# Rebuilding split weights on one core: the low words shifted in place by GpSimd, one VectorE operation per half weight instead of two, and a new order

## The chip, the core and the metric

The kernel runs on one core of a Trainium2 chip. The metric is device time in microseconds for one launch. The engines have short names in what follows: PE is TensorE (matrix products), DVE is VectorE, ACT is ScalarE, POOL is GpSimd and SP is SyncE, which only starts transfers. A transfer that ACT starts stands in ACT's own instruction order.

## The reference: what is computed

Clustered attention feeds a feed-forward block. There are 4 batches of 8 heads, 768 positions, head width 64, and 16 centroids per head. A query sees only the keys whose nearest centroid is its own.

```python
mask   = q_assign[:, :, :, None] == k_assign[:, :, None, :]      # nearest centroid
scores = where(mask, q @ k.T / sqrt(64), -1e9)
attn   = softmax(scores) @ v                                     # 4 x 8 x 768 x 64
x      = attn.transpose(0, 2, 1, 3).reshape(3072, 512)
h      = x @ w_in                                                # 512 x 2048
out    = (h * tanh(softplus(h))) @ w_out                         # 2048 x 512
```

## The kernel before, in words

**Order.** All work is cut into small named steps. A class `Plan` (line 27) collects each step with a due time, sorts by it and issues the steps; a step first calls `pl.after(...)` and so issues what it needs (lines 40 to 53). Due times and the shares of the engines come from a table of numbers `T` at line 812. A tile scheduler then lays each engine's instructions in a row from what the steps issue, and `in_turn` (line 102) keeps the table's order for some of ACT's steps. So a changed number in the table can move instructions on every engine.

**Weights.** Each of the two weight matrices arrives as 64-bit values whose two 32-bit words hold one weight between them. They come in 32 halves of 128 x 512 values, numbers 0 to 15 from `w_in` and 16 to 31 from `w_out`. For each half:

- `w_load` (line 213) brings the half into a staging tile `stage`.
- `w_abs` (ACT, line 239) reads the high words and writes a first form of the weight as float32 into a tile `w`.
- `w_f32` (DVE) finishes the float32 in two operations: line 248 shifts `w` left by 3 bits, and line 249 takes the low words, shifts them right by 29 and ORs them in.
- `w_sq` (PE, line 264) sums squares with four products into the tile `gram`.

When all 16 halves of a matrix are in `gram`, `w_scale` (line 270) works out one scale, `ws0r` for `w_in` and `ws1r` for `w_out`, through a short chain on DVE and PE (lines 184, 192 and 195 to 201). Only then can `w_hi` (line 278) multiply each of the 8 tiles of a matrix by the scale, on POOL at line 285 or on ACT at line 287 as the table's share `f_ws` says, and round it to float16 on POOL at line 288. `w_lo` (line 290) subtracts the rounded value from the scaled one on POOL at line 297, which gives the low float16 part. A few tiles go through ACT and DVE at lines 282 and 295 instead.

**Attention.** There are 32 heads in three blocks of 256 queries, each block worked in two halves. PE makes the scores `s` (lines 488 and 493), DVE takes the row maximum `m` (line 503), ACT the exponential `p` (line 510), and DVE or POOL finishes the row sum `l` (lines 520 and 521). In the first eight heads PE transposes `p` (line 549), DVE or ACT copies it out of PSUM (lines 568 and 570), and PE multiplies by the values (line 588). In later heads POOL makes the float16 high part `hl` (line 539), DVE the low part (line 556), a DMA transposes both, and PE multiplies (line 598).

Each head is prepared first. `prep_hi` (line 366) makes the tile `A` from `qk`: either ACT (line 378) or POOL (line 376) does it with the scale inside, or POOL scales `qk` in place first (line 373). `prep_lo` (line 380) makes `B`, the rest, on POOL by a subtraction when `qk` was scaled in place (line 384), otherwise on DVE (line 386). The shares `f_a` and `f_b` decide. Copies `T`, `Z`, `B` and `A` follow, by ACT (line 396) or by DMA (line 398). Line 426 is PE's product with the centroids.

**Feed-forward.** PE multiplies `x` by the float16 weights (lines 655 to 657), ACT makes `u` (line 665), POOL and DVE the two parts of `g` (lines 669 and 677), and PE multiplies by the second matrix (lines 693 to 695). PE takes these pieces between those of the attention.

Of the kernel before, what the change touches and what calls it, by code (L numbers as in the profile page):

```python
# [55 lines left out]
def tile_clustered_attention_mish_ffn(  # L56
# [9 lines left out]
    nc = tc.nc  # L66
# [5 lines left out]
    op1 = pool("operands1", 1)  # L72
# [135 lines left out]
    stage = {}  # L208
# [34 lines left out]
    def w_f32(n):  # L243
        pl.after(("w_abs", n))
        i, hf = divmod(n, 2)
        words = stage[n].bitcast(U32).rearrange("p (n t) -> p n t", t=2)
        f = W[i + 1].bitcast(U32)[:, hf * 512 : (hf + 1) * 512]
        nc.vector.tensor_scalar(f, f, 3, None, op0=ALU.logical_shift_left)
        nc.vector.scalar_tensor_tensor(
            f, words[:, :, 0], 29, f, op0=ALU.logical_shift_right, op1=ALU.bitwise_or  # L250
        )

    def w_sq(n):

# [481 lines left out]
    for n in range(32):  # L736
        p = n // 16
        t = T["w0", p] + T["w_d", p] * (n % 16)
        pl.at(t - T["w_l", p], w_load, n)
        pl.at(t, w_abs, n)  # L740
        pl.at(t + 0.2, w_f32, n)
        pl.at(t + 0.4, w_sq, n)
    for i in range(16):
        p = i // 8
        t = T["w0", p] + T["w_d", p] * 15 + T["ws0", p]
# [56 lines left out]
    for k in range(12):  # L802
        for a in range(2):
            for f in range(8):
                pl.at(ffn(8 * k + 4 * a + f / 2 + T["m2"]), m2, k, a, f)
            t = 8 * k + 4 * a + 4 + T["m2"]
# [3 lines left out]


T = {
    ('f_ws', 0): 0.5,
    ('f_ws', 1): 0.5,
    'direct': 2,
    't0': 2.1861,
    ('f_pl', 0): 0.5,
# [10 lines left out]
    ('dq', 'copy_a'): 0,  # L828
    ('f_copy_t', 0): 0,
    ('f_copy_z', 0): 0.567,  # L830
    ('f_copy_b', 0): 0,
    ('f_copy_a', 0): 0,
    ('f_copy_t', 1): 3,
    ('f_copy_z', 1): 0.874,
    ('f_copy_b', 1): 0,
    ('f_copy_a', 1): 0.193,
    ('f_a', 0): 1,
    ('f_a', 1): 0.239,
    ('f_b', 0): -1,
    ('f_b', 1): 0,  # L840
    'prep_hi': 3.0343,
    'prep_lo': 1.1321,
    'copy_t': 0.5952,
    'copy_z': 0.8008,
    'copy_b': 3.5728,
# [1 line left out]
    'hot_copy': 0.979,  # L847
    'm_store': 0.3296,
    ('f_l', 0): 0,
    ('f_l', 1): 0.434,  # L850
    ('w_l', 0): 0.8888,
    ('w_l', 1): 0.7772,
    'v0': 1.5,
    'v_d': 0.4275,
    ('q_hi', 0): 0.8,
    ('q_lo', 0): 1.4045,
# [5 lines left out]
    ('f_w', 1): 0.363,  # L862
    'lead': 0.5333,
    'units0': 24,
    ('f_d', 0): 0.965,
    ('f_d', 1): 0.732,
    ('f_lo', 0): 0,
    ('f_lo', 1): 0,
    ('f_hi', 0): 0,
    ('f_hi', 1): 1,  # L870
    'grp': 2,
    'mish': 0,
    'O': 1,
    'off0': 25.401,
    'pace': 1.0,
    ('span', 0): 1.1575,
    ('span', 1): 1.0762,
    ('load', 0): -3.8837,
    ('load', 1): 2.8849,
    ('w0', 0): 0.89,  # L880
    ('w0', 1): 9.896,
    ('w_d', 0): 0.3597,
    ('w_d', 1): 0.1964,
    ('ws0', 0): 4.1159,
    ('ws0', 1): 1.7919,
# [6 lines left out]
    'put': 2.3669,  # L892
    ('scores', 0): 0.4,
    ('rowmax', 0): 0.9821,
    ('expo', 0): 2.0645,
    ('recip', 0): 0.7,
    ('scores', 1): 1.8591,
    ('rowmax', 1): 1.6368,
# [41 lines left out]
```

## Time and profile before

The median of three runs is 977.86 us, from 976.33 to 979.1.

| of the profiled execution | |
|---|---|
| its own time | 978.06 us |
| span in the trace | 976.3 us |
| mean granted TensorE clock | 0.981 |
| start of the first product of the feed-forward (line 655) | 208.18 us after the span's start |

Times of a row are microseconds from the span's start unless a unit says otherwise. In a table of windows, each engine has its busy time and its count of instructions in brackets, and `PEclk` is the part of full speed that PE was granted. In a group of instructions stand the line, the engine, the operation and the tiles as out<-in; then the total busy time, the mean of one in nanoseconds, and the idle time just before them with what ended it. In a timeline a row is the start, the length, the instruction, how many of it follow each other, and in square brackets the idle time before it and what ended that.

### The profile page before, as it was taken

Reading aid. Unit: us, or ns where it says so; the run is one execution under the profiler, and the core shown is the slowest. Engines: PE = TensorE matmul, PEld = TensorE weight load, DVE = VectorE, ACT = ScalarE, POOL = GpSimd, SP = SyncE. Lnnn points to the kernel's source line nnn. Section 1 sums busy time; section 2 is a strip of 40 time slices with the busy share of each in tenths; the row PEclk is TensorE's granted clock in tenths of the full one; section 3 lists DMA queues with packets and bytes.
Section 4 is the critical chain, followed back from the end, with each engine's and each line's share of the span. In section 5 each row is a group of like instructions: output and inputs, shape, how many; then the busy total and the mean of one; then the engine's idle time right before and its main releaser. Section 6 shows DMA issues by size and latency. Waiting matters only on the chain. (4 is left out here: it accounts for less than half of the span.)

```text
span 976.3 us, 17239 instructions
## 1 busy us (share of the span) xinstructions
PE 918.5 (94%) x6481; PEld 676.3 (69%) x6481; DVE 644.9 (66%) x1162; ACT 562.2 (58%) x938; POOL 410.0 (42%) x543
## 2 busy tenths in 40 slices
PE   3997789999999999999999999999999999999998
PEld 3765567777667767767777767676777777666663
DVE  6988987887777667866776667866777676211010
ACT  3776367767766656566676665557666665211111
POOL 3226679644444335535434334434434344211010
PEclk9999779999999999999999999999999999999999
DMA  9733732266777866767867667666577565100000
GB/s 360 236 96 90 207 92 61 70 114 129 140 146 138 151 118 139 141 122 148 129 139 134 155 124 144 111 130 142 122 139 123 116 117 111 31 12 22 12 12 21
DMA packets 250323, 115.85 MB, mean 119 GB/s; under 512 B 229632, under 2 KB 229632, under 8 KB 250240
## 3 DMA queue, kind: packets, MB, share of 16 engines
q1 hardware_dynamic: 238272, 82.50, 43.2%
q10 hardware_dynamic: 11968, 32.25, 12.0%
q8 instruction: 51, 0.84, 0.4%
q14 instruction: 32, 0.26, 0.1%
HBM read 35.68 MB, written 6.29 MB: 43 GB/s over the span
## 5 line engine op out<-in xcount | busy, mean ns | idle before, releaser
L510 ACT ACTIVATE p<-s,m 128x768 f32<-128x768 f32 x192 | 172.8, 900 | 132.6 <-DVE m L503 101.7
L656 PE MATMUL h<-x,w 128*128 128x256 f16 x768 | 209.7, 273 | 0.6 <-POOL x L637 0.6
L655 PE MATMUL h<-x,w 128*128 128x256 f16 x768 | 210.1, 274 | 0.1
L657 PE MATMUL h<-x,w 128*128 128x256 f16 x768 | 210.1, 274 | 0.0
L556 DVE SCALAR_TENSOR_TENSOR hl<-p,l,hl 128x768 f16<-128x768 f32 x144 | 152.3, 1058 | 72.7 <-POOL hl L539 72.4
L503 DVE TENSOR_REDUCE m<-s 128x1 f32<-128x768 f32 x192 | 181.2, 946 | 10.0 <-PE s L493 8.4
L539 POOL TENSOR_SCALAR hl<-p,l 128x768 f16<-128x768 f32 x144 | 132.7, 922 | 125.2 <-ACT p L510 47.5
L677 DVE SCALAR_TENSOR_TENSOR g<-u,mscg,g 128x512 f16<-128x512 f32 x96 | 75.8, 792 | 139.8 <-POOL g L669 139.0
L669 POOL TENSOR_SCALAR g<-u,mscg 128x512 f16<-128x512 f32 x96 | 80.8, 842 | 173.7 <-ACT u L665 149.0
L693 PE MATMUL O<-w,g 128*128 128x512 f16 x384 | 146.8, 382 | 2.9 <-POOL g L669 2.1
L695 PE MATMUL O<-w,g 128*128 128x512 f16 x384 | 146.2, 381 | 0.4 <-DVE g L677 0.4
L694 PE MATMUL O<-w,g 128*128 128x512 f16 x384 | 146.2, 381 | 0.0
L488 PE MATMUL s<-A,B 128*128 128x384 f32 x384 | 123.3, 402 | 14.9 <-ACT p L510 12.7
L665 ACT ACTIVATE u<-h,msch 128x512 f32<-128x512 f32 x96 | 65.7, 687 | 97.9 <-PE h L657 94.6
L493 PE MATMUL s<-Z,T 80*128 80x384 f32 x384 | 101.3, 345 | 2.8 <-ACT T L467 2.8
L598 PE MATMUL o<-pt,v 128*128 128x256 f16 x864 | 102.7, 273 | 0.6 <-DMA pt<-hl 0.4
L520 POOL TENSOR_SCALAR l<-l 128x1 f32<-128x1 f32 x129 | 40.5, 314 | 142.7 <-ACT p L510 139.5
L598 PEld LDWEIGHTS <-v 128*128 128x128 f16 x864 | 83.8, 98 | 16.6 <-issue 1.7
L655 PEld LDWEIGHTS <-w 128*128 128x128 f16 x768 | 75.2, 98 | 20.6 <-issue 6.0
L488 PEld LDWEIGHTS s<-A,B 128*128 128x128 f32 x384 | 64.1, 194 | 33.5 <-ACT p L510 18.5
L656 PEld LDWEIGHTS <-w 128*128 128x128 f16 x768 | 75.2, 98 | 15.5 <-issue 1.4
L657 PEld LDWEIGHTS <-w 128*128 128x128 f16 x768 | 75.2, 98 | 15.0 <-issue 5.4
(184 smaller groups left out, 1324.0 us busy)
## 6 DMA issues: line engine op xcount, KB each, us to landing
qk<-in_qk_dram ACTq DMA_DIRECT2D x32, 384.0 KB, 4.2
stage<-in_w_out_dram ACTq DMA_DIRECT2D x16, 512.0 KB, 4.0
vraw<-in_vP_dram SPq DMA_DIRECT2D x16, 384.0 KB, 4.5
out_dram<-osb SPq DMA_DIRECT2D x24, 256.0 KB, 2.7
B<-T ACTq DMA_DIRECT2D x30, 192.0 KB, 4.3
A<-A SPq DMA_DIRECT2D x25, 192.0 KB, 4.8
stage<-in_w_in_dram SPq DMA_DIRECT2D x8, 512.0 KB, 8.9
stage<-in_w_in_dram ACTq DMA_DIRECT2D x8, 512.0 KB, 4.5
```

What stands on the lines that cost most here:

```text
L488: nc.tensor.matmul(s[:, j, :384], st["B", n][:, q0 : q0 + P], st["A", n][:, j * 384 : (j + 1) * 384], start=True, stop=False,)
L503: nc.vector.tensor_reduce(m, st["s", i, a][:, :, :384], axis=AX.XY, op=ALU.max, negate=True)
L510: in_turn(nc.scalar.activation(p.rearrange("p (n x) -> p n x", n=2), st["s", i, a][:, :, :384], AF.Exp, bias=st["m", i, a], scale=1.0, acc ...
L539: nc.gpsimd.tensor_scalar(t[:, 0], p, r, 1.0, op0=ALU.mult, op1=ALU.mult)
L556: nc.vector.scalar_tensor_tensor(t[:, 1], p, r, t[:, 0], op0=ALU.mult, op1=ALU.subtract)
L598: nc.tensor.matmul(o[:, s * 256 : s * 256 + 256], vst[b, h // 2][:, c, h % 2].rearrange("p g d -> p (g d)"), st["pt", 2 * m + s][:, :, c + ...
L655: nc.tensor.matmul(o, wh, xh, start=(c == 0), stop=False)
L656: nc.tensor.matmul(o, wh, xl, start=False, stop=False)
L657: nc.tensor.matmul(o, wl, xh, start=False, stop=(c == 3))
L693: nc.tensor.matmul(o, gh, wh, start=(f == 0 and fi == 0), stop=False)
L694: nc.tensor.matmul(o, gh, wl, start=False, stop=False)
L695: nc.tensor.matmul(o, gl, wh, start=False, stop=(f == 7 and fi == 1))
```

## The change

In `w_f32` POOL now works on the low words in place, in the staging tile, as integers read and written through a multiply and a minimum: each low word is multiplied by 2 to the minus 29, which leaves its upper three bits, and limited to 7. DVE then makes the float32 in one operation that shifts `f` left by 3 and ORs in the low words. The lines after 250 have a number one lower than before.

```diff
     def w_f32(n):
         pl.after(("w_abs", n))
         i, hf = divmod(n, 2)
-        words = stage[n].bitcast(U32).rearrange("p (n t) -> p n t", t=2)
+        low = stage[n].bitcast(U32).rearrange("p (n t) -> p n t", t=2)[:, :, 0]
         f = W[i + 1].bitcast(U32)[:, hf * 512 : (hf + 1) * 512]
-        nc.vector.tensor_scalar(f, f, 3, None, op0=ALU.logical_shift_left)
-        nc.vector.scalar_tensor_tensor(
-            f, words[:, :, 0], 29, f, op0=ALU.logical_shift_right, op1=ALU.bitwise_or
-        )
+
+        nc.gpsimd.tensor_scalar(low, low, 2.0**-29, 7.0, op0=ALU.mult, op1=ALU.min)
+        nc.vector.scalar_tensor_tensor(f, f, 3, low, op0=ALU.logical_shift_left, op1=ALU.bitwise_or)
...
 T = {
-    ('f_ws', 0): 0.5,
-    ('f_ws', 1): 0.5,
+    ('f_ws', 0): 0.061,
+    ('f_ws', 1): 1,
...
-    ('f_b', 1): 0,
+    ('f_b', 1): 1,
```

The table has some twenty changed numbers in all. What they do to the counts of instructions:

| work | before | after |
|---|---|---|
| DVE operations that finish the float32 of a half | 64 | 32 |
| POOL operations on low words | 0 | 32 |
| scaling of `w_in` tiles: POOL, ACT | 4, 4 | 0, 8 |
| scaling of `w_out` tiles: POOL, ACT | 3, 3 | 6, 0 |
| `qk` scaled in place on POOL (line 373) | 8 | 32 |
| `A` from `qk`: POOL with the scale inside, ACT | 6, 18 | 0, 24 |
| `B`: POOL (line 384), DVE (line 386) | 8, 24 | 32, 0 |
| `B` copied: ACT, DMA | 0, 30 | 6, 24 |
| row sums (line 520): POOL, DVE | 129, 63 | 150, 42 |

PE has the same products, and in nearly the same order from the first product of the feed-forward on.

The first place is DVE where the first `w_out` halves become float32, beside the attention of the first batch. `stage` is the half with its two words per weight, `w` its float32. Before:

```order
L248 TENSOR_SCALAR w_1060<-w_1060 128x512
L249 SCALAR_TENSOR_TENSOR w_1060<-stage_1019,w_1060 128x512
L568 COPY pt_998<-q_0_3_994 128x384
L503 TENSOR_REDUCE m_0_1172<-s_0_1167 128x1
L248 TENSOR_SCALAR w_1060<-w_1060 128x512
L503 TENSOR_REDUCE m_1_1216<-s_1_1211 128x1
L249 SCALAR_TENSOR_TENSOR w_1060<-stage_1021,w_1060 128x512
L248 TENSOR_SCALAR w_1097<-w_1097 128x512 x2
L521 RECIPROCAL l_1_1073<-l_1_1073 128x1
L249 SCALAR_TENSOR_TENSOR w_1097<-stage_1033,w_1097 128x512
```

After, at the corresponding place:

```order
L502 TENSOR_REDUCE m_0_1199<-s_0_1194 128x1
L567 COPY pt_898<-q_1_3_1036 128x384
L250 SCALAR_TENSOR_TENSOR w_1111<-w_1111,stage_1029 128x512
L502 TENSOR_REDUCE m_1_1245<-s_1_1240 128x1
L567 COPY pt_1065<-q_0_3_1061 128x384
L250 SCALAR_TENSOR_TENSOR w_1111<-w_1111,stage_1045 128x512
L567 COPY pt_990<-q_1_3_1167 128x384
L250 SCALAR_TENSOR_TENSOR w_1178<-w_1178,stage_1079 128x512
```

The shifts are gone from the row, one operation per half is left, and it reads a low word that POOL has written.

The second place is POOL at the same time in the program, from where the first scale is known. Before:

```order
L285 TENSOR_SCALAR w_323<-w_323,ws0r 128x1024
L285 TENSOR_SCALAR w_490<-w_490,ws0r 128x1024
L285 TENSOR_SCALAR w_603<-w_603,ws0r 128x1024
L285 TENSOR_SCALAR w_760<-w_760,ws0r 128x1024
L288 TENSOR_SCALAR w_275<-w_276 128x1024
L520 TENSOR_SCALAR l_1_1073<-l_1_1073 128x1
L297 TENSOR_TENSOR w_275<-w_276,w_275 128x1024
L288 TENSOR_SCALAR w_276<-w_323 128x1024
L297 TENSOR_TENSOR w_276<-w_323,w_276 128x1024
```

After, where the first float16 weight is made:

```order
L249 TENSOR_SCALAR stage_1238<-stage_1238 128x512
L383 TENSOR_TENSOR B_1226<-qk_1081,A_1173 128x768
L249 TENSOR_SCALAR stage_1259<-stage_1259 128x512
L519 TENSOR_SCALAR l_1_1339<-l_1_1339 128x1
L249 TENSOR_SCALAR stage_1269<-stage_1269 128x512
L287 TENSOR_SCALAR w_275<-w_276 128x1024
L249 TENSOR_SCALAR stage_1288<-stage_1288 128x512
L372 TENSOR_SCALAR qk_1430<-qk_1430,scq 128x768
L296 TENSOR_TENSOR w_275<-w_276,w_275 128x1024
```

POOL scaled and rounded `w_in` while the `w_out` halves were being finished; now its work on the `w_out` halves stands ahead of the first rounding, and the scaling is not in its row.

The third place is ACT, where it multiplies the `w_in` tiles by `ws0r`. Before:

```order
L510 ACTIVATE p_0_1042,l_0_1043<-s_0_1035,m_0_1040 128x768
L239 ACTIVATE w_1060<-stage_1019 128x512
L398 DMA B_1003<-T_975 64x768
L287 ACTIVATE w_276<-w_276,ws0r 128x1024
L287 ACTIVATE w_428<-w_428,ws0r 128x1024
L510 ACTIVATE p_1_1072,l_1_1073<-s_1_1065,m_1_1070 128x768
```

After, from the second of the eight scalings to the next exponential (ahead of the first scaling stands another exponential):

```order
L286 ACTIVATE w_401<-w_401,ws0r 128x1024
L286 ACTIVATE w_475<-w_475,ws0r 128x1024
L286 ACTIVATE w_561<-w_561,ws0r 128x1024
L286 ACTIVATE w_673<-w_673,ws0r 128x1024
L286 ACTIVATE w_740<-w_740,ws0r 128x1024
L286 ACTIVATE w_839<-w_839,ws0r 128x1024
L286 ACTIVATE w_926<-w_926,ws0r 128x1024
L227 DMA stage_1288<-in_w_out_dram 128x512
L239 ACTIVATE w_1343<-stage_1269 128x512
L569 COPY pt_1212<-q_1_0_1376 128x384
L239 ACTIVATE w_1343<-stage_1288 128x512
L509 ACTIVATE p_0_1407,l_0_1408<-s_0_1400,m_0_1405 128x768
```

The scalings on ACT were four, in two pairs with an exponential between; now they are eight, in one block, and the last two line 239 of `w_out` and a copy stand between the block and the next exponential.

More of the change, by code (lines that the diff above doesn't have):

```diff
@@ L830 @@
     ('f_copy_z', 0): 0.567,
-    ('f_copy_b', 0): 0,
+    ('f_copy_b', 0): 1,
     ('f_copy_a', 0): 0,
     ('f_copy_t', 1): 3,
-    ('f_copy_z', 1): 0.874,
+    ('f_copy_z', 1): 0.994,
     ('f_copy_b', 1): 0,
@@ L837 @@
     ('f_a', 0): 1,
-    ('f_a', 1): 0.239,
+    ('f_a', 1): 0,
     ('f_b', 0): -1,
-    ('f_b', 1): 0,
+    ('f_b', 1): 1,
     'prep_hi': 3.0343,
-    'prep_lo': 1.1321,
+    'prep_lo': 2.673,
     'copy_t': 0.5952,
@@ L849 @@
     ('f_l', 0): 0,
-    ('f_l', 1): 0.434,
-    ('w_l', 0): 0.8888,
+    ('f_l', 1): 0.294,
+    ('w_l', 0): 1.4353,
     ('w_l', 1): 0.7772,
-    'v0': 1.5,
+    'v0': 1.214,
     'v_d': 0.4275,
@@ L864 @@
     'units0': 24,
-    ('f_d', 0): 0.965,
+    ('f_d', 0): 0.566,
     ('f_d', 1): 0.732,
@@ L868 @@
     ('f_lo', 1): 0,
-    ('f_hi', 0): 0,
+    ('f_hi', 0): 0.425,
     ('f_hi', 1): 1,
@@ L875 @@
     'pace': 1.0,
-    ('span', 0): 1.1575,
+    ('span', 0): 1.634,
     ('span', 1): 1.0762,
     ('load', 0): -3.8837,
-    ('load', 1): 2.8849,
+    ('load', 1): 2.8855,
     ('w0', 0): 0.89,
-    ('w0', 1): 9.896,
-    ('w_d', 0): 0.3597,
+    ('w0', 1): 9.386,
+    ('w_d', 0): 0.5318,
     ('w_d', 1): 0.1964,
-    ('ws0', 0): 4.1159,
-    ('ws0', 1): 1.7919,
+    ('ws0', 0): 4.606,
+    ('ws0', 1): 1.1124,
     ('ws1', 0): -0.216,
@@ L894 @@
     ('rowmax', 0): 0.9821,
-    ('expo', 0): 2.0645,
+    ('expo', 0): 1.3834,
     ('recip', 0): 0.7,
```

## Prediction

> **What bounds the kernel now.** I read the page first, for the share of each engine and the slices of the span.
>
> ```profile
> PE 918.5 (94%) x6481; PEld 676.3 (69%) x6481; DVE 644.9 (66%) x1162; ACT 562.2 (58%) x938; POOL 410.0 (42%) x543
> PE   3997789999999999999999999999999999999998
> PEclk9999779999999999999999999999999999999999
> ```
>
> PE is at nine tenths nearly everywhere. The exceptions are the first slice and slices 4 to 6, each 24.4 us long, where the granted clock dips too. I cut that part into windows, beside the steady part and the end.
>
> ```profile
> 86.00:98.00 12.00, 6.38 (x52) 4.15 (x48) 9.78 (x15) 9.15 (x15) 10.96 (x10) 0.93 0.42 111
> 98.00:104.00 6.00, 3.73 (x26) 3.17 (x27) 5.89 (x10) 2.45 (x5) 2.56 (x3) 0.56 0.61 206
> 104.00:116.00 12.00, 9.50 (x79) 6.53 (x77) 12.00 (x15) 4.17 (x8) 10.82 (x9) 1.00 0.66 199
> 116.00:128.00 12.00, 8.21 (x38) 6.66 (x38) 10.97 (x18) 7.07 (x14) 7.35 (x8) 0.54 0.79 215
> 128.00:140.00 12.00, 10.43 (x80) 7.54 (x78) 11.87 (x18) 6.43 (x13) 6.97 (x8) 0.89 0.31 84
> 140.00:208.20 68.20, 65.09 (x458) 50.42 (x459) 56.78 (x125) 50.54 (x100) 49.61 (x60) 0.97 0.27 66
> 208.20:830.00 621.80, 608.75 (x4364) 454.93 (x4364) 446.23 (x773) 407.19 (x649) 274.06 (x360) 1.00 0.69 132
> ```
>
> The columns are PE, weight loads, DVE, ACT, POOL, then clock and DMA. From 208 us on PE is busy 98% (608.75 of 621.8) at full clock. Between 86 and 140 us it is not: DVE is busy 50.51 of 54 us, and PE has the clock at 0.54 to 0.56 in 18 of them. What PE waits for there, from the view of waits between 86 and 141 us:
>
> ```profile
> PE gram L264 <- DVE w L249: 13.8, 7, 3.7
> ```
>
> So in this stage DVE's float32 conversion of the `w_out` halves ends last. The groups of DVE in that window, and then the same two lines from 0 to 86 us:
>
> ```profile
> L249 DVE SCALAR_TENSOR_TENSOR w<-stage,w 128x512 uint32<-128x512 uint32 x16 | 19.0, 1195 | 0.1
> L248 DVE TENSOR_SCALAR w<-w 128x512 uint32<-128x512 uint32 x16 | 17.1, 1075 | 1.1 <-ACT w L239 1.0
> ...
> L249 DVE SCALAR_TENSOR_TENSOR w<-stage,w 128x512 uint32<-128x512 uint32 x16 | 11.5, 718 | 0.1
> L248 DVE TENSOR_SCALAR w<-w 128x512 uint32<-128x512 uint32 x16 | 8.5, 533 | 0.4
> ```
>
> The same 32 operations cost 36.1 us here and 20.0 us there. The timelines of DVE, POOL and PE show why:
>
> ```profile
> 30.40 0.43 DVE L248 TENSOR_SCALAR w<-w 128x512 uint32<-128x512 uint32 x1
> 30.86 0.69 DVE L249 SCALAR_TENSOR_TENSOR w<-stage,w 128x512 uint32<-128x512 uint32 x1
> 94.10 2.01 DVE L249 SCALAR_TENSOR_TENSOR w<-stage,w 128x512 uint32<-128x512 uint32 x1
> 96.03 3.51 DVE L248 TENSOR_SCALAR w<-w 128x512 uint32<-128x512 uint32 x2
> 93.44 2.12 POOL L297 TENSOR_TENSOR w<-w,w 128x1024 f16<-128x1024 f32 x1
> 97.10 2.17 POOL L297 TENSOR_TENSOR w<-w,w 128x1024 f16<-128x1024 f32 x1
> 100.27 0.61 PE L264 MATMUL gram<-w 128*128 128x128 bf16 x4 [3.66 <-DVE w L249]
> ```
>
> The first two rows are the bare prices, 0.43 and 0.69 us. Beside POOL's subtraction of 2.1 us the same lines take 2.01 and 1.76 us (3.51 for two). PE then stands 3.66 us, and the window from 98 us has the clock at 0.56.
>
> **What the change is worth, part by part.** The sum is made against the profiled execution, 978.06 us, of which the span is 976.3; it lies 0.2 us above the median of the runs.
>
> *The stage of the `w_out` halves.* PE's full-clock work from 86 to 140 us is its busy time times the clock: 6.38 x 0.93 + 3.73 x 0.56 + 9.50 x 1.00 + 8.21 x 0.54 + 10.43 x 0.89 = 31.2 us of 54. The loss is 22.8 us. After the change DVE has 50.51 - 36.1 = 14.4 us of other work there and 16 operations of the kind of line 249. At the bare 0.69 us they make 11.0 us, and DVE needs 25.4 us where PE needs 31.2; even at 1.0 us each DVE needs 30.4. What makes them dear now, POOL's scaling and rounding of `w_in`, stands behind POOL's work on the halves in the new order, as the second place of the order shows. So PE ends last there and the loss goes: -22.8 us. If half of it stays, since DVE has other work in bursts, the gain is 11.4; this is one bound.
>
> *POOL's new operation.* 32 of 128 x 512 with a stride of two words; the trace of before has none. Its rows of elementwise work on POOL are these:
>
> ```profile
> L669 POOL TENSOR_SCALAR g<-u,mscg 128x512 f16<-128x512 f32 x96 | 80.8, 842 | 173.7 <-ACT u L665 149.0
> L373 POOL TENSOR_SCALAR qk<-qk,scq 128x768 f32<-128x768 f32 x8 | 7.2, 905 | 14.6 <-PE as L426 12.1 <-DMA qk<-in_qk_dram 2.4
> L384 POOL TENSOR_TENSOR B<-qk,A 128x768 fp32r<-128x768 f32 x8 | 15.3, 1913 | 0.3
> ```
>
> By size line 373 gives 905 x 512 / 768 = 603 ns from below and line 384 gives 1275 ns from above. I take 0.75 us between the two, nearer to line 669 (0.842), which has the same size. 32 x 0.75 = 24 us, 12 for each matrix. In the `w_out` stage POOL loses at least the scaling and rounding, so it is covered: 0. If the cover is gone, DVE waits 12 us there; that is a rival below.
>
> The Trainium skill, page "GPSIMD Engine Reference", section "8. Key points", says that for elementwise work DVE is structurally about twice as fast. By that an operation on POOL would take 2 x 0.43 = 0.86 us, an estimate, and the sum would be the same as long as POOL is not what ends last.
>
> *ACT's block of eight.* This is a new wait. The order has the eight multiplications by `ws0r` in one piece, with two line 239 and one copy before the next exponential; nothing else on ACT can pass. The rows of ACT for these:
>
> ```profile
> L287 ACT ACTIVATE w<-w,ws0r 128x1024 f32<-128x1024 f32 x4 | 4.4, 1148 | 2.1 <-DMA Z<-B 2.1
> L239 ACT ACTIVATE w<-stage 128x512 f32<-128x512 f32 x32 | 20.9, 671 | 2.2 <-DMA stage<-in_w_out_dram 2.2
> L510 ACT ACTIVATE p<-s,m 128x768 f32<-128x768 f32 x192 | 172.8, 900 | 132.6 <-DVE m L503 101.7
> L570 ACT COPY pt<-q 128x384 f32<-128x384 f32 x48 | 22.8, 475 | 17.0 <-DVE onehot L456 8.0 <-PE o L588 5.1 <-PE q L549 3.2
> ```
>
> 8 x 1.148 + 2 x 0.671 + 0.475 + 0.900 = 11.9 us. Ahead of it ACT waits for `ws0r`, whose DVE chain has a row maximum (0.95), a copy (0.55), a conversion and small operations between its steps, which I put at 4 us to 5.5 us: ACT gives no exponential for about 16.5 us. PE has, in its order in that time, the square sums of five tiles, two score pairs, twelve transposes and six products with the centroids. The means of these groups between 86 and 208 us:
>
> ```profile
> L549 PE MATMUL q<-ident,p 128*128 128x128 f32 x183 | 31.3, 300 | 1.8 <-DVE pt L568 1.7
> L488 PE MATMUL s<-A,B 128*128 128x384 f32 x62 | 19.4, 395 | 1.3 <-ACT p L510 1.3
> L493 PE MATMUL s<-Z,T 80*128 80x384 f32 x62 | 16.8, 354 | 0.0
> L264 PE MATMUL gram<-w 128*128 128x128 bf16 x64 | 7.5, 248 | 13.8 <-DVE w L249 13.8
> L426 PE MATMUL as<-C,qk 128*128 128x128 f32 x60 | 9.1, 310 | 1.4 <-ACT p L510 1.4
> ```
>
> By busy time over count: 36 to 40 square products at 0.117 = 4.5, four score products at 0.313 and four at 0.271 = 2.3, twelve transposes at 0.171 = 2.1, six at 0.152 = 0.9: about 10 us. PE stands for some 6.5 us, 9 where the chain is longer, and the clock then costs more. Before, each loss on PE of 3.66 us was followed by a window of 6 us at 0.56, where 3.73 x 0.44 = 1.6 us go; with several waits I take 3. I set the whole at +12, with bounds 0 (PE has more queued than I count) and +17 (nothing but the clock recovers).
>
> *The start.* ACT's first line 467 stands behind a load:
>
> ```profile
> 19.80 0.98 ACT L467 ACTIVATE T<-oh,mbi,msc 16x768 fp32r<-16x768 bf16 x1 [10.80 <-DMA vraw<-in_vP_dram]
> 20.84 1.26 PE L493 MATMUL s<-Z,T 80*128 80x384 f32 x4 [2.80 <-ACT T L467]
> ```
>
> In the new order that load no longer stands ahead. At most PE's 2.80 us go; POOL's subtraction, which ends with it, holds some. I take -1.5 us, between 0 and -2.8.
>
> *The steady part.* For each of 22 later heads POOL gains a scaling and a subtraction, 0.905 + 1.913 = 2.82 us, 62 us in all. POOL is busy 274 of 621.8 us, so 348 are free. DVE loses line 386 and ACT gains some copies, but PE is busy 98% there: 0, with a loss as a rival.
>
> The sum: -22.8 + 12 - 1.5 = -12.3, and 978.06 - 12.3 = 965.8; I say **966 us**. The first product of line 655 then starts near 196 us, not at 208.18.
>
> **Rivals.**
>
> *ACT's block is covered.* PE's queue is long enough, since PE takes scores of the next blocks meanwhile. For it: from 86 to 208 us PE stood only 1.3 us ahead of line 488 for `p`, with four scalings on ACT in that time. Then 978.06 - 22.8 - 1.5 = 953.8 us, **954**. Chance 0.16.
>
> *POOL takes back what DVE saves.* The 16 new operations on POOL beside the conversions hold up DVE's remaining one, as line 297 does now; 16 x 0.75 = 12 us, which with the block on ACT uses up the gain: 965.8 + 12 = 977.8, **978**, no change. For it: line 248 takes up to 1.76 beside POOL and 0.43 alone. Against it: line 249, which reads two tensors, costs 0.718 in the mean up to 86 us. Chance 0.15. By the Trainium skill, page "GPSIMD Engine Reference", section "8. Key points", POOL shares its SBUF interfaces with DVE, with contention for DVE operations in a 2-port mode or with two inputs in SBUF; the rows at 94.10 and 96.03 us agree, 2.01 for 0.69 and 1.76 for 0.43.
>
> *Slower: POOL's queue in the steady part.* The scaling and the subtraction stand in POOL's row ahead of the float16 parts of the probabilities (line 539), on which DVE already waits:
>
> ```profile
> L556 DVE SCALAR_TENSOR_TENSOR hl<-p,l,hl 128x768 f16<-128x768 f32 x144 | 152.3, 1058 | 72.7 <-POOL hl L539 72.4
> ```
>
> Its point of decision: 12.3 us over 22 heads is 0.56 us per head of 2.82, a fifth. Where a third of the 62 us reaches PE, 20.7 us, the time is 965.8 + 20.7 = **986 us**. Against it: PE has waited at 98% busy with DVE standing those 72 us. Chance 0.16.
>
> **How the numbers follow.** The forecast has 0.53, its own range 957 to 975 (the block from +3 to +17, the start's bounds, part of the stage's loss left). The range over all cases goes from 952, a little below the first rival, to 980, past the second; what is left out is the third and the lower edge, under 0.2. What a measurement of this kernel can tell from no change is 0.3%, 2.9 us: faster is below 975. Faster: 0.53 + 0.16 = 0.69, less a little for the forecast's upper edge, 0.68. Same: the second rival and that edge, 0.16. Slower: 0.16.
>
> **What would show it.** Right: line 250 at 0.7 to 0.8 us in the `w_out` halves, `gram` waiting for it under 4 us, a block of 9.2 us on ACT with a wait of PE for `p` of 6 us or more behind it, line 655 starting by 198 us, and from there to the end the same 768 us. Wrong: PE in the steady part under 97% with waits on `hl` or `B` (third rival); line 250 over 1.2 us (second); no wait behind ACT's block (first).

## The result, and the profile after

The change made the kernel slower: 988.43 us in the median (987.15 to 994.34, four runs) against 978.48 us of the kernel before beside it. The ratio is 1.0117, with a 95% interval of 1.0092 to 1.0141. The forecast was 966 us with a range of 952 to 980. The profiled execution took 987.43 us, with a span of 985.6. The first product of line 655 (now 654) starts at 209.12 us, for 208.18 before and about 196 in the forecast; from there to the end it is 776.5 us, for 768.1 before.

The first part of the page of the kernel after, and its slices:

```profile
PE 918.4 (93%) x6481; PEld 675.1 (68%) x6481; DVE 624.1 (63%) x1091; ACT 573.6 (58%) x954; POOL 541.9 (55%) x631
PE   4898669998999999999999999899999999999997
PEclk8799889999999999999999999999999999999999
POOL 8985888997654546754555456544645544111010
```

PE has the same work (918.4 us, 918.5 before). POOL went from 410.0 to 541.9 us and is now at eight or nine tenths in nearly all of the first ten slices. To find the 9.3 us by which the span grew, the span is cut into five stages. PE's loss in a stage is its length minus busy time times granted clock. Windows of the kernel before, then of the kernel after, with the columns in the same order as in the prediction. The clock has two digits, which matters over 510 us: in the kernel before it is 0.97 from 340 to 390 us, in the kernel after 1.00. So the table takes its last row of the kernel before in two windows (50 - 47.88 x 0.97, and 460 - 453.25 for the rest at full clock):

```profile
0.00:86.00 86.00, 65.00 (x445) 50.52 (x447) 69.63 (x165) 50.30 (x100) 28.38 (x63) 0.94 0.63 207
86.00:140.00 54.00, 38.25 (x271) 28.05 (x267) 50.51 (x72) 29.27 (x54) 38.66 (x34) 0.81 0.55 158
140.00:190.00 50.00, 47.38 (x331) 36.75 (x332) 39.30 (x92) 36.12 (x73) 41.73 (x48) 0.97 0.19 49
190.00:340.00 150.00, 145.33 (x1072) 110.99 (x1069) 113.69 (x197) 105.43 (x173) 63.31 (x90) 1.00 0.74 139
340.00:850.00 510.00, 501.13 (x3565) 371.27 (x3564) 354.60 (x618) 321.89 (x515) 223.36 (x289) 1.00 0.66 126
...
340.00:390.00 50.00, 47.88 (x328) 34.85 (x327) 34.48 (x65) 30.81 (x51) 21.61 (x30) 0.97 0.65 126
```

```profile
0.00:86.00 86.00, 66.51 (x448) 51.64 (x448) 62.56 (x140) 52.18 (x101) 68.81 (x81) 0.90 0.59 199
86.00:140.00 54.00, 38.14 (x276) 29.51 (x274) 36.58 (x83) 37.76 (x64) 42.57 (x35) 0.87 0.50 151
140.00:190.00 50.00, 46.63 (x341) 35.03 (x336) 33.12 (x73) 32.67 (x68) 45.98 (x49) 1.00 0.19 48
190.00:340.00 150.00, 139.48 (x1010) 105.06 (x1011) 114.36 (x184) 101.41 (x167) 97.76 (x110) 0.99 0.68 133
340.00:850.00 510.00, 497.27 (x3548) 369.14 (x3546) 358.80 (x589) 328.95 (x526) 269.78 (x335) 1.00 0.66 127
```

| PE's loss, us | before | after | difference |
|---|---|---|---|
| 0 to 86 | 24.9 | 26.1 | +1.2 |
| 86 to 140 | 23.0 | 20.8 | -2.2 |
| 140 to 190 | 4.0 | 3.4 | -0.6 |
| 190 to 340 | 4.7 | 11.9 | +7.2 |
| 340 to 850 | 10.3 | 12.7 | +2.4 |

The differences add up to 8.0 of the 9.3 us; the rest lies behind 850 us and in the rounding. Two things stand out. From 86 to 140 us DVE has 13.9 us less to do (36.58 for 50.51) and PE loses nearly as much as before. And the loss comes after 190 us, where the forecast had none.

The groups of POOL's new operation, over the whole run, and of DVE's one from 86 to 141 us:

```profile
L249 POOL TENSOR_SCALAR stage<-stage 128x512 uint32<-128x512 uint32 x32 | 65.2, 2039 | 6.3 <-DMA stage<-in_w_out_dram 3.0 <-DMA stage<-in_w_in_dram 1.0
L250 DVE SCALAR_TENSOR_TENSOR w<-w,stage 128x512 uint32<-128x512 uint32 x16 | 12.6, 790 | 1.8 <-POOL qk L372 1.7
```

DVE's operation costs 0.79 us, as forecast (0.7 to 0.8). POOL's costs 2.04 us where 0.75 was taken, and 65.2 us in all instead of 24.

The block on ACT, with PE's wait behind it; the two rows of ACT are the eight scalings. The rows of POOL and DVE at that time stand below them:

```profile
118.55 4.25 ACT L286 ACTIVATE w<-w,ws0r 128x1024 f32<-128x1024 f32 x4
122.71 4.25 ACT L286 ACTIVATE w<-w,ws0r 128x1024 f32<-128x1024 f32 x4
127.23 2.12 POOL L296 TENSOR_TENSOR w<-w,w 128x1024 f16<-128x1024 f32 x1
127.61 2.30 DVE L250 SCALAR_TENSOR_TENSOR w<-w,stage 128x512 uint32<-128x512 uint32 x1 [1.68 <-POOL qk L372]
129.96 0.61 PE L263 MATMUL gram<-w 128*128 128x128 bf16 x4 [3.64 <-DVE w L250]
```

Line 239 of the last two halves stands behind the block (the first of them ends at 127.52 us, nearest to DVE's start, though the profile names POOL's line 372, which ended at 127.27), DVE behind it, and PE behind DVE: 3.64 us. But the block is only a part of this wait: DVE's operation took 2.30 us instead of 0.69 beside POOL's subtraction, so 1.6 of the 3.64 us are POOL's.

Last, the chain that makes the first scale: the row maximum of line 184, PE's product of line 192, and the reciprocal, at which the scale is known. The last row is the last subtraction that makes float16 weights. Before, then after:

```profile
74.99 0.16 DVE L184 TENSOR_REDUCE ws0m<-wss 128x1 f32<-128x16 f32 x1
...
80.36 0.28 PE L192 MATMUL ws0p<-ws0m,ones 128*128 128x1 f32 x2
...
86.64 0.16 DVE L201 RECIPROCAL ws0r<-ws0r 128x1 f32<-128x1 f32 x1
...
186.14 2.38 POOL L297 TENSOR_TENSOR w<-w,w 128x1024 f16<-128x1024 f32 x1
```

```profile
88.99 0.16 DVE L184 TENSOR_REDUCE ws0m<-wss 128x1 f32<-128x16 f32 x1
...
111.28 0.35 PE L192 MATMUL ws0p<-ws0m,ones 128*128 128x1 f32 x2 [0.32 <-DVE xf L628]
...
115.90 0.17 DVE L201 RECIPROCAL ws0r<-ws0r 128x1 f32<-128x1 f32 x1
...
223.65 2.58 POOL L296 TENSOR_TENSOR w<-w,w 128x1024 f16<-128x1024 f32 x1
```

The scale comes 29 us later, and the weights' float16 parts end at 226.2 us and not at 188.5. Of the 29 us, 14 are the row maximum, which comes later. The rest comes from the place of its product in PE's row: line 192 starts 22.3 us behind the maximum, for 5.4 before. With POOL's operation in the short form and the same rows (h1, below) it starts 21.2 us behind, at 112.25 after 91.01 us, so this belongs to the new order and not to POOL's price. No run moves that product.

The float16 work now runs beside the first feed-forward and the first later heads. From 190 to 240 us it holds up a DVE operation on the values (line 332), which took 1.00 us at 194.01 and takes 2.88 beside POOL's subtraction:

```profile
196.77 2.13 POOL L296 TENSOR_TENSOR w<-w,w 128x1024 f16<-128x1024 f32 x1
...
196.83 2.88 DVE L332 SCALAR_TENSOR_TENSOR v<-vraw,vs1r,v 128x768 f16<-128x768 f32 x1 [0.43 <-POOL v L331]
```

DVE's operation on the probabilities (line 555) is longer there too, 1.43 us in the mean for 1.04. But its long ones stand beside other work of POOL; the longest, 2.57 us, is beside line 383, the subtraction for a later head.

### The profile page after: what moved, and what is told of

Read it like the earlier page. It is cut to its first block, busy times and chain, and to the rows that moved or that the text cites. A ratio compares the mean times of both kernels' runs of the same rounds, so it can differ in the third digit from the quotient of the medians.

```text
span 985.6 us, 17186 instructions
## 1 busy us (share of the span) xinstructions
PE 918.4 (93%) x6481; PEld 675.1 (68%) x6481; DVE 624.1 (63%) x1091; ACT 573.6 (58%) x954; POOL 541.9 (55%) x631
## 5 line engine op out<-in xcount | busy, mean ns | idle before, releaser
L555 DVE SCALAR_TENSOR_TENSOR hl<-p,l,hl 128x768 f16<-128x768 f32 x144 | 158.5, 1102 | 74.6 <-POOL hl L538 74.2
L502 DVE TENSOR_REDUCE m<-s 128x1 f32<-128x768 f32 x192 | 181.3, 946 | 22.5 <-PE s L492 20.8
L668 POOL TENSOR_SCALAR g<-u,mscg 128x512 f16<-128x512 f32 x96 | 77.8, 811 | 173.3 <-ACT u L664 153.4
L676 DVE SCALAR_TENSOR_TENSOR g<-u,mscg,g 128x512 f16<-128x512 f32 x96 | 78.3, 818 | 143.8 <-POOL g L668 143.7
L519 POOL TENSOR_SCALAR l<-l 128x1 f32<-128x1 f32 x150 | 52.9, 353 | 101.2 <-ACT p L509 94.6
L656 PEld LDWEIGHTS <-w 128*128 128x128 f16 x768 | 75.3, 98 | 13.8 <-issue 4.0
```

The source lines that it names most:

```text
L502: nc.vector.tensor_reduce(m, st["s", i, a][:, :, :384], axis=AX.XY, op=ALU.max, negate=True)
L555: nc.vector.scalar_tensor_tensor(t[:, 1], p, r, t[:, 0], op0=ALU.mult, op1=ALU.subtract)
L656: nc.tensor.matmul(o, wl, xh, start=False, stop=(c == 3))
```

## The experiments

The first theories were these. A: POOL's operation was mis-sized, and a POOL that is full up to 130 us costs the time. B: POOL's scaling and subtraction for the later heads cost it. C: ACT's block of eight costs it. D, added with the second set: the new order costs it, whatever the operation costs. Theories E to G stand in the expectations.

All results, each with its ratio to the kernel before on the same chip:

| run | median, us | ratio, 95% interval |
|---|---|---|
| the kernel after | 988.43 | 1.0117, 1.0092 to 1.0141 |
| e1_short_op | 990.38 | 1.0110, 1.0090 to 1.0131 |
| e2_order_alone | 995.64 | 1.0177, 1.0154 to 1.0199 |
| e3_op_alone | 995.57 | 1.0161, 1.0137 to 1.0185 |
| h1_after_held_short | 988.64 | 1.0112, 1.0094 to 1.0129 |
| h2_before_held_min | 1015.80 | 1.0380, 1.0357 to 1.0403 |
| h3_before_held_mul | 977.79 | 0.9997, 0.9984 to 1.0011 |
| h4_before_held_out | 976.53 | 0.9983, 0.9968 to 0.9998 |
| h5_after_heads_on_dve | 987.65 | 1.0088, 1.0063 to 1.0113 |
| h6_after_block_split | 991.06 | 1.0125, 1.0105 to 1.0144 |
| h7_before_loads_on_sp | 976.50 | 0.9982, 0.9968 to 0.9997 |
| h8_after_all_three | 991.08 | 1.0129, 1.0107 to 1.0151 |
| t1_before_tiny_convert | 968.00 | 0.9883, 0.9863 to 0.9903 |
| t3_before_no_load_wait | 977.71 | 0.9985, 0.9971 to 1.0000 |
| t4_before_both | 963.84 | 0.9842, 0.9810 to 0.9873 |
| b1_before_heads_on_pool | 1004.19 | 1.0254, 1.0230 to 1.0278 |
| r1_after_no_load_wait | 985.08 | 1.0063, 1.0046 to 1.0081 |
| r2_before_out_sp | 976.64 | 0.9974, 0.9960 to 0.9989 |

Nine of these seventeen runs lie outside every range that was set for them: e1, e2, e3, h2, h6, h8 and b1 above the highest, t1 and t4 between two.

### First set: the operation, the order, and the operation's forms

e1_short_op:

```diff
-        nc.gpsimd.tensor_scalar(low, low, 2.0**-29, 7.0, op0=ALU.mult, op1=ALU.min)
-        nc.vector.scalar_tensor_tensor(f, f, 3, low, op0=ALU.logical_shift_left, op1=ALU.bitwise_or)
+        nc.gpsimd.tensor_scalar(low[:, :192], low[:, :192], 2.0**-29, 7.0, op0=ALU.mult, op1=ALU.min)
+        nc.vector.scalar_tensor_tensor(f, f, 3, low, op0=ALU.logical_shift_left, op1=ALU.bitwise_and)
```

> POOL's operation works on 192 of the 512 low words, and DVE's operation ANDs where it ORed, so that every value stays finite: the weights are not the reference's, DVE's operation has the same size, and POOL's costs about 2.04 x 192 / 512 = 0.77 us, the size that the prediction had taken. Theory A (the POOL operation was mis-sized, and POOL full up to 130 us is what costs the time): most of the loss goes, 962 to 976 us. Theory B (POOL's scaling and subtraction of the later heads costs the time): little changes, 982 to 990 us. Theory C (the order with ACT's block of eight costs it): 980 to 988.

e2_order_alone is the kernel after with the old body of `w_f32`; e3_op_alone is the kernel before with the new one.

> The new table with the old two DVE operations and no POOL operation. Theory A: POOL is free again, so near the kernel before or a little better, 970 to 982 us. Theory B: the later heads still load POOL, 983 to 990. Theory C: the block of eight is still there and DVE has its old load, 985 to 995.

> The old table with the new pair of operations. Theory A: POOL has 65 us more in a stage of 140 us in which it had 67 us of work, which leaves it nearly full and delays the scaling and rounding of the weights: 980 to 995 us. Theory B: the later heads are as before, so 965 to 979. Theory C: no block of eight, 965 to 979.

All three are slower than the kernel before by 1.1 to 1.8%, and the first is no faster than the kernel after. But a change in an operation's length also moves the order that the scheduler lays, so each of these changes two things at once. They refute no theory by themselves; they show that the new table is slower still without its operation (e2), and the old table slower with it (e3), each in the order that the scheduler then lays.

p1_forms (one execution, so its total time is not compared) adds to the kernel before, on a tile `z` of 128 x 1024 words whose contents are no weights, six rounds of:

```diff
+        G(ue, ue, 2.0**-29, 7.0, op0=ALU.mult, op1=ALU.min)      # L823
+        G(uc, uc, 2.0**-29, 7.0, op0=ALU.mult, op1=ALU.min)      # L824, no stride
+        G(e, e, 1.0, 7.0, op0=ALU.mult, op1=ALU.min)             # L825, float32
+        G(c, c, 1.0, 7.0, op0=ALU.mult, op1=ALU.min)             # L826, float32, no stride
+        G(c, c, 1.0, 1.0, op0=ALU.mult, op1=ALU.mult)            # L827
+        G(o, ue, 2.0**-29, 7.0, op0=ALU.mult, op1=ALU.min)       # L828, not in place
+        G(uo, e, 2.0**-29, 7.0, op0=ALU.mult, op1=ALU.min)       # L829
+        G(ue, ue, 2.0**-29, 1.0, op0=ALU.mult, op1=ALU.mult)     # L830
```

> The kernel before with 48 POOL operations of 128 x 512 at its end, six of each of eight forms, which only lengthen its tail. It asks what makes the operation cost 2.04 us: integers, the stride of two words, the minimum, or the work in place. If integers: 32-bit integer forms about 2 us at either stride and float forms 0.6 to 0.9. If the stride: strided forms about 2 us in both types. If the minimum: only the form with two multiplications is short.

Its groups on POOL from 940 us on:

```profile
L828 POOL TENSOR_SCALAR z<-z 128x512 f32<-128x512 uint32 x6 | 12.1, 2020 | 0.5
L825 POOL TENSOR_SCALAR z<-z 128x512 f32<-128x512 f32 x6 | 11.8, 1972 | 0.5
L829 POOL TENSOR_SCALAR z<-z 128x512 uint32<-128x512 f32 x6 | 11.8, 1969 | 0.5
L826 POOL TENSOR_SCALAR z<-z 128x512 f32<-128x512 f32 x6 | 11.5, 1920 | 0.5
L823 POOL TENSOR_SCALAR z<-z 128x512 uint32<-128x512 uint32 x5 | 10.2, 2032 | 0.4
L824 POOL TENSOR_SCALAR z<-z 128x512 uint32<-128x512 uint32 x5 | 9.6, 1920 | 0.4
L830 POOL TENSOR_SCALAR z<-z 128x512 uint32<-128x512 uint32 x6 | 3.9, 644 | 0.5
L827 POOL TENSOR_SCALAR z<-z 128x512 f32<-128x512 f32 x6 | 3.7, 620 | 0.4
```

It is the minimum. Every form that has it takes 1.92 to 2.03 us, integers or not, with a stride or without; the two with a second multiplication take 0.62 and 0.64. Other operations in its place were not measured.

### Second set: one thing at a time, in a held order

To change an operation's length and nothing else, the program is built twice. The first build is the kernel as it is, and each engine's row is noted; in the second, with the edit, every instruction waits for its predecessor in that row:

```python
for engine, names in ORDER.items():          # rows of the first build
    names = [n for n in names if n in made and str(made[n].engine) == engine]
    for x, y in zip(names, names[1:]):
        tc.add_manual_dep(made[y], x, no_sync, reason="held order")
```

An instruction that the edit moves to another engine is placed there by the scheduler; all others stay where they were. Such runs are called held. The code above is shortened. No run holds the rows without any edit; h3 and t3, held on the kernel before, lie within 0.2% of it.

h1_after_held_short, on the kernel after:

```diff
-        nc.gpsimd.tensor_scalar(low, low, 2.0**-29, 7.0, op0=ALU.mult, op1=ALU.min)
+        nc.gpsimd.tensor_scalar(low, low, 2.0**-29, 1.0, op0=ALU.mult, op1=ALU.mult)
```

> The kernel after, with each engine's row of instructions held exactly as it is, and only the limit to 7 replaced by a multiplication by 1, which the probe of forms measured at 0.64 us in place of 2.0; a low word may round up to 8, which changes a weight's last bits. Theory A (the POOL operation was mis-sized): POOL has some 44 us less before 130 us, so most of the loss goes, 962 to 978 us. Theory D (the new order costs the time whatever the operation costs): 983 to 990 us.

h2_before_held_min and h3_before_held_mul, on the kernel before, and h4_before_held_out, which does it for `n >= 16` alone (shortened; `low` is `words[:, :, 0]`):

```diff
-        nc.vector.tensor_scalar(f, f, 3, None, op0=ALU.logical_shift_left)
-        nc.vector.scalar_tensor_tensor(f, low, 29, f, op0=ALU.logical_shift_right, op1=ALU.bitwise_or)
+        nc.gpsimd.tensor_scalar(low, low, 2.0**-29, 7.0, op0=ALU.mult, op1=ALU.min)   # h2
+        nc.gpsimd.tensor_scalar(low, low, 2.0**-29, 1.0, op0=ALU.mult, op1=ALU.mult)  # h3, h4
+        nc.vector.scalar_tensor_tensor(f, f, 3, low, op0=ALU.logical_shift_left, op1=ALU.bitwise_or)
```

> The kernel before with every engine's row held, except that DVE's shift of each half is left out and POOL's operation with the limit to 7 is put in, at 2.0 us. So the operation alone, without the new table. Theory A: 65 us more on POOL ahead of its scaling and rounding; the halves come at POOL's pace, 980 to 1000 us. Theory D: DVE's gain shows, 960 to 976 us.

> As the run before it, with the operation of 0.64 us (a multiplication by 1 in place of the limit). Theory A and the prediction's own sum without the block on ACT: 953 to 968 us. Theory D: the same as the run before it, 960 to 976 us. If POOL's queue for the weights is what counts, no better than 976 us.

> As the run before it, with the change made to the 16 halves of w_out alone; those of w_in keep DVE's two operations. If the stage from 86 to 140 us is all that the change is worth, the same as the run before it, within 3 us. If the first 86 us count too, the two differ: later here if DVE's load there matters, earlier here if POOL's does.

In the old order the operation alone costs 37 us (h2), and with the short form nothing (h3). So its size matters there. In the new order it does not: h1 gives 988.64, the same as the kernel after. Theory A falls for the kernel after, and D stands. With the short form on the halves of `w_out` alone (h4) the time is 1.3 us from that of h3, so the halves of `w_in` matter little there. POOL's 32 operations take 65.2 us in h2, as in the kernel after. Its first window shows where most of the 37 us lie:

```profile
0.00:86.00 86.00, 50.30 (x287) 38.61 (x287) 41.91 (x106) 34.11 (x66) 57.66 (x66) 0.76 0.53 184
```

PE loses 86 - 50.30 x 0.76 = 47.8 us up to 86 us, against 24.9. The rest lies from 140 to 190 us (50 - 38.12 x 0.78 = 20.3 us, against 4.0). In the new order this price does not show, as h1 says, and the order has one of its own.

The result of h3 was a surprise too: DVE is spared its shifts and the kernel gains nothing. DVE's group from 86 to 141 us, and then the window:

```profile
L254 DVE SCALAR_TENSOR_TENSOR w<-w,stage 128x512 uint32<-128x512 uint32 x16 | 20.0, 1271 | 0.1
```

```profile
86.00:140.00 54.00, 38.83 (x271) 28.36 (x271) 37.78 (x57) 30.26 (x56) 46.68 (x46) 0.84 0.51 160
```

DVE's remaining operation takes 1.27 us in the mean, POOL is busy 46.7 of 54 us, and PE's loss in the stage is nearly as it was (54 - 38.83 x 0.84 = 21.4 us, for 23.0). This is the outcome of the second rival, in the old order, but hardly by its mechanism. The sixteen operations took 9 us more than at 0.69 each, and the longest, 2.62 us, stand beside the subtraction of the `w_in` weights that was there before. Two are held by the new operation of POOL alone, by half a microsecond each (1.16 us at 108.71 and 1.15 at 128.87).

### Third set: the heads, the block, the loads

h5_after_heads_on_dve, held, for `n >= H` (the later heads):

```diff
-            nc.gpsimd.tensor_scalar(r, r, scq, 1.0, op0=ALU.mult, op1=ALU.mult)
+            nc.gpsimd.memset(idle, 0.0)                      # 128 x 1, keeps the place
...
-            nc.gpsimd.tensor_tensor(Bt, r, A, op=ALU.subtract)
+            nc.vector.scalar_tensor_tensor(Bt, r, scq, A, op0=ALU.mult, op1=ALU.subtract)
```

> The kernel after with every row held, except for the 24 later heads: POOL's scaling of qk becomes a write of 128 x 1, ACT's first form takes the scale, and the second part is made by DVE as in the kernel before. Theory E (POOL's 2.9 us per later head cost what PE lost after 190 us, 24.6 us against 15.2 in the kernel before): 977 to 982 us. Theory F (the float16 weights, made on POOL up to 225 us and not 188, cost that): 985 to 989 us.

h6_after_block_split, held, with ACT's row edited in one place:

```diff
     L509 exponential
     L286 x2
-    L286 x6
     L227 DMA, L239, L569, L239, L509 exponential
+    L286 x2
     ... L509 exponential
+    L286 x2
     ... L509 exponential
+    L286 x2
```

> The kernel after with every row held, but ACT's block of eight scalings taken apart: two, then the two line 239, the copy and the exponential, then two behind each of three exponentials. If the block costs what PE lost from 116 to 140 us, 12.6 us: 975 to 981 us. If POOL's conversion of the weights or the loop of the loads holds that stretch anyway: 984 to 989 us.

h7_before_loads_on_sp is h3 with `nc.sync` as the queue of the `w_out` loads; h8_after_all_three joins h1, h5 and h6.

> As the run of the kernel before with the short operation on all halves (977.8 us), with the loads of w_out issued by SP instead of ACT. Theory G (what holds the stage from 86 to 140 us is a ring of waits: a load waits in ACT's row for a staging buffer, which DVE frees, and ACT's exponentials wait behind it): 958 to 970 us. If the ring is closed elsewhere, by POOL's float16 work and DVE's operation beside it: 975 to 980 us.

> The kernel after, rows held, with the short operation, the later heads on DVE and the block of eight split. If the three costs add up (the short operation 0 by itself, the heads 6 to 10, the block 8 to 12): 966 to 975 us. If they cover each other: 976 to 983 us. If neither is the cause: 985 to 989 us.

None of the four does what a single cause would. Splitting the block gains nothing (991.06), and PE loses 24 - 13.27 x 0.70 = 14.7 us from 116 to 140 us, for 12.6 with the block. So Theory C falls as far as the block goes; the eight scalings stay on ACT in h6, and no run takes four of them back. Theory G falls too: with the loads on SP (h7) the time is 976.50, in the range that was set for a ring closed elsewhere. The three edits together (h8) give 991.08, no better than h6 alone. Taking the later heads off POOL does what it should after 340 us and loses it again before. Its two windows:

```profile
190.00:340.00 150.00, 140.17 (x980) 106.20 (x980) 116.41 (x187) 100.54 (x164) 79.45 (x100) 0.94 0.65 126
340.00:850.00 510.00, 500.94 (x3585) 372.95 (x3584) 359.05 (x613) 333.51 (x530) 222.09 (x320) 1.00 0.66 129
```

After 340 us the loss is 9.1 us, about as in the kernel before (10.3), for 12.7 in the kernel after. From 190 to 340 us it is 150 - 140.17 x 0.94 = 18.2 us, for 11.9. A reason that no run isolates: DVE has the operations back in a stretch where POOL's late subtractions are beside it. What remains is a difference in the median that the intervals do not separate (987.65 and 988.43).

### Fourth set: what the conversion and the heads are worth in the old order

All four are held, on the kernel before. t1_before_tiny_convert and t3_before_no_load_wait, for `n >= 16`; t4_before_both is both:

```diff
+            f, words = f[:, :16], words[:, :16]                            # t1, in w_f32
...
+            hi = ones.unsqueeze(1).to_broadcast([P, 4, P])                 # t3, in w_abs
...
+            low = ones.bitcast(U32).unsqueeze(1).to_broadcast([P, 4, P])   # t3, in w_f32
```

> The kernel before, rows held, with both of DVE's operations on the 16 w_out halves made on 16 of 512 columns, so w_out is left unfinished in the rest: DVE's price there is nearly gone. If DVE's conversion is what holds PE from 86 to 140 us, as the prediction had it: 955 to 966 us. If the halves come late for other reasons (loads, ACT's row): 973 to 979 us.

> The kernel before, rows held, with DVE's full operations, but ACT and DVE read a resident tile of ones in place of the 16 staged w_out halves: the loads still run and nothing waits for them, and they wait for no buffer; w_out is left out of the result. If the ring of load, buffer and ACT's row holds the stage: 958 to 968 us. If DVE's time holds it: 974 to 980 us.

> Both at once: no wait for the loads and DVE's operations on 16 columns. It bounds what any faster conversion of w_out could bring in this order. If loads and DVE share the blame: 952 to 962 us, better than either. If neither matters, and POOL's scaling and the attention's own chain hold the stage: 972 to 980 us.

With DVE's operations on 16 columns the kernel gains 1.2% (968.00), with the loads out of the way as well 1.6% (963.84), which the intervals just fail to separate, and with the loads alone nearly nothing. But t1 does not take DVE's price away. Its groups from 86 to 141 us:

```profile
L253 DVE TENSOR_SCALAR w<-w 128x16 uint32<-128x16 uint32 x16 | 9.3, 586 | 4.8 <-ACT w L242 4.7
L254 DVE SCALAR_TENSOR_TENSOR w<-stage,w 128x16 uint32<-128x16 uint32 x16 | 8.1, 513 | 0.1
```

The 32 operations still take 17.4 us of 36.1, since many stand waiting beside POOL (last section). Taking 18.7 us from DVE took PE's loss from 86 to 140 us from 23.0 to 54 - 44.99 x 0.87 = 14.9 us. So a part of the stage was DVE's, as the forecast said, and shown by this run; what the conversion would be worth if all its time went, t1 does not say. In this order operations of a thirty-second of the size bring 11.7 us, or 15.8 with the loads out of the way, and not 22.8.

b1_before_heads_on_pool is the reverse of h5: the later heads' scaling and subtraction on POOL, in the old order. That order is taken from a build with a POOL operation of 128 x 1 where the scaling will stand, the scheduler places the subtraction, and POOL keeps the six `A` of later heads that the kernel after gives to ACT.

> The kernel before, rows held, with the 24 later heads' scaling and subtraction on POOL as in the kernel after, and DVE's operation left out. The prediction's sum: no change, 976 to 980 us. The prediction's third rival with a third of the 62 us reaching PE: 995 to 1000 us. From PE's losses after 190 us in the kernel after against the kernel before: 982 to 988 us.

It costs 24.5 us (1004.19 against 979.67), somewhat more than the third rival's 20.7. Its window after 340 us:

```profile
340.00:850.00 510.00, 486.29 (x3416) 356.50 (x3415) 352.20 (x595) 314.16 (x503) 265.14 (x316) 1.00 0.63 124
```

PE loses 23.7 us there, for 10.3 in the kernel before. POOL is busy only half of the time (265 of 510 us).

### Last set

r1_after_no_load_wait is h1 with t3's edit, and with a write of 128 x 1 for POOL's operation on `w_out`. r2_before_out_sp is h4 with the `w_out` loads on SP.

> The kernel after, rows held, with the short operation for w_in; for the 16 halves of w_out POOL's operation is a write of 128 x 1 and ACT and DVE read a resident tile of ones, so that nothing waits for the loads; w_out is left out of the result. Beside the run of the kernel after with the short operation (988.6 us). If the waits for the loads hold the stage in the new order: 972 to 980 us. If not, 984 to 989 us.

> The kernel before, rows held, with the new pair of operations for w_out alone, POOL's in the short form, and the loads of w_out on SP: the two edits that each gave about 0.2%. If they add: 973 to 976 us, 0.3 to 0.5% faster than before. If they have the same cause: 976 to 978 us.

In the new order the waits for the loads, with POOL's operation on `w_out`, are worth about half a per cent (1.0063 against 1.0112 of h1); more than half of the loss stays. r2 is 0.26% faster than the kernel before (0.9974, 0.9960 to 0.9989). Its interval overlaps those of h4 and h7, so whether the two edits add is not shown; 976.64 lies in the range for one cause.

## Why the prediction was wrong, point by point

The sum was 965.8 us and the profiled execution took 987.43, 21.6 us more. From 86 to 140 us the sum had -22.8 for the stage and +12 for the block, -10.8 together, and the table above has -2.2: 8.6 us of the miss. The start gives 2.7 us (-1.5 against +1.2), and the stretch after 140 us, put at nothing, 9.0; the rest is rounding and what lies behind 850 us. So two steps failed: the loss of the `w_out` stage did not go, and the work that was moved was not free later.

**"So PE ends last there and the loss goes: -22.8 us."** This step failed. PE's loss from 86 to 140 us went from 23.0 to 20.8 us. The wait that the forecast named did shrink (PE for DVE's `w`, 13.8 before):

```profile
PE gram L263 <- DVE w L250: 6.3, 3, 3.6
PE s L492 <- DMA T<-stg: 2.9, 1, 2.9
PE q L548 <- ACT p L509: 2.1, 2, 1.3
```

Others took its place, a few microseconds each. The sum had compared DVE's work with PE's (25.4 us against 31.2) and given the whole loss back. That would hold if only total work counted, and it does not: DVE is busy 36.6 of 54 us after the change, and PE still loses 20.8. In the old order t1 measures 11.7 us, by the two medians, for half of DVE's time on the 16 halves. The reason given for DVE's low price also held only in part: POOL's subtraction does stand beside the last halves (2.30 us at 127.61), since the first float16 weight is made before the last halves are done. And the 1.76 us that the prediction calls the most line 248 takes is a mean of two; the second of them took 2.33.

**"I take 0.75 us."** The lower bound (0.603) was the price of a multiplication, and it was right for that form (0.62 to 0.64). The operation has a minimum, which no row of the trace had, and took 2.04 us, above the upper bound of 1.275. Its 41 us more (65.2 instead of 24) are not always hidden: h2 shows 37 us in the old order. In the new order this term moves nothing (h1), so the slower result is not put down to it alone.

**"I set the whole at +12."** From 116 to 140 us PE lost 12.6 us in the kernel after, and the exponential did stand behind eight scalings. That this is the size of the forecast is chance: the kernel before lost 24 - 8.21 x 0.54 - 10.43 x 0.89 = 10.3 us in the same stretch, and PE did not wait 6 us for `p` there but 1.3 at a time at most, and 3.64 for DVE. h6 says the same: without the block the time is 991.06.

**"I take -1.5 us" for the start.** PE lost 1.2 us more up to 86 us, not less. The wait that was to go is still there: ACT's line 466 again stands behind a load (7.13 us, by the profile the one of `vraw`), and PE waits 4.17 us for it, for 2.80 before.

**"0, with a loss as a rival" for the steady part.** After 340 us PE lost 2.4 us more. In h5 it lost 9.1 us there in place of 12.7, so this part goes with POOL's work for the later heads. From 190 to 340 us it lost 7.2 us more. The trace puts this beside the float16 weights that end 38 us later, and h5 does not take it back; no run tried the weights alone, so it is argued and not shown. The forecast had taken it for a gain that this work "stands behind" the halves, and had not asked what it would then stand beside.

**The rivals.** The slower one, POOL's queue in the steady part, had a chance of 0.16 and a time of 986 us, near to the measured 988.43. Its mechanism is real: 24.5 us in the old order (b1), where a third of 62 us, 20.7, had been supposed. In the kernel after it accounts for the few microseconds after 340 us and at most a part of the 7.2 before, and taking the work off POOL (h5) does not make the kernel faster clear of the noise. PE is busy 601.5 of 620.9 us from 209 to 830 us, 96.9%, where the sign was under 97%, and `hl` and `B` are not among its waits. So the rival's time was near by luck, for the larger part. The second, POOL taking back what DVE saves, has its outcome in h3 and little of its mechanism. The first, the block covered, is not what happened either: PE waits behind the block, and the -22.8 that its 954 us rest on did not come.

What stays open: why the new order loses 20.8 us from 86 to 140 us. DVE has time to spare there (36.6 of 54 us), and the short operation, the split block, the heads on DVE and the loads each move the whole by 5 us at most. The rows wait for each other in turn, and no single wait was found to hold them. What no run tried is the place of the scale's product in PE's row, which delays the block, the rounding and the subtractions together.

## What to carry to other kernels

A stage in which one engine is busy 94% of the time can still be held by the order of all of them: before giving a loss back in full, make that engine's operation tiny in a held order and see what the stage is worth, and look in the trace whether it became tiny in time too. An engine that is half idle on average is not free, if its row stands between two others: 2.9 us per head on POOL cost 24.5 us at 52% busy (b1). And an operation whose form no row shows is not bounded by the rows of other forms: 2.04 us lay above the costliest of them, 1.275 by size. It has to be timed first.

## What the runs showed of the hardware

The price of POOL's operation with a minimum was new: 1.92 to 2.03 us for 128 x 512, in both types and with or without the stride, against 0.62 (float32, no stride) and 0.64 (uint32, stride) with a multiplication.

The other surprise is how DVE is slowed by POOL. In t1 an operation of 16 columns sometimes takes longer than one of 512 alone. Its DVE rows, then POOL's:

```profile
93.48 2.02 DVE L253 TENSOR_SCALAR w<-w 128x16 uint32<-128x16 uint32 x1 [1.48 <-ACT w L242]
...
100.85 0.17 DVE L253 TENSOR_SCALAR w<-w 128x16 uint32<-128x16 uint32 x1
...
93.34 2.13 POOL L302 TENSOR_TENSOR w<-w,w 128x1024 f16<-128x1024 f32 x1
```

Alone it takes 0.17 us. Started 0.14 us after POOL's subtraction of two tensors, it takes 2.02 and ends with it, at 95.50 and 95.47 us: it waits for POOL's operation to end and is not slowed in proportion. The same wait shows beside a POOL operation with one input. In the kernel after, POOL's scaling of `qk` and DVE's line 555, which takes 1.02 us alone:

```profile
353.85 0.91 POOL L372 TENSOR_SCALAR qk<-qk,scq 128x768 f32<-128x768 f32 x1
...
353.91 1.65 DVE L555 SCALAR_TENSOR_TENSOR hl<-p,l,hl 128x768 f16<-128x768 f32 x1 [1.03 <-POOL hl L538]
```

Beside POOL's operation with the minimum it depends on the moment. Rows of the kernel after, then of h2, POOL's and DVE's:

```profile
94.78 1.99 POOL L249 TENSOR_SCALAR stage<-stage 128x512 uint32<-128x512 uint32 x1
...
95.35 0.69 DVE L250 SCALAR_TENSOR_TENSOR w<-w,stage 128x512 uint32<-128x512 uint32 x1
```

```profile
164.20 2.00 POOL L253 TENSOR_SCALAR stage<-stage 128x512 uint32<-128x512 uint32 x1
...
164.23 1.15 DVE L254 SCALAR_TENSOR_TENSOR w<-w,stage 128x512 uint32<-128x512 uint32 x1
```

Started 0.57 us after POOL's, DVE's operation on two tensors keeps its bare 0.69 us. Started 0.03 us after it, it takes 1.15, and still ends 0.8 us before POOL's. So here DVE waits, if at all, for the first part of the 2 us only; how long that part is, no run was made to measure. That fits DVE's 0.79 us in the mean in the kernel after.

The Trainium skill, page "GPSIMD Engine Reference", section "8. Key points", has contention between the two engines for DVE instructions in a 2-port mode or with two inputs in SBUF. The second trace agrees, 1.65 us for 1.02 with two inputs; the third, 0.69 us beside a POOL operation, does not. Whether the operation of the first is in such a mode no trace shows.
